# The first stage as one fixed list of named operations, with key reciprocals in PSUM, norms in place and block sums taken from PSUM

## The chip, the cores and the metric

The kernel runs on one core of one Trainium2 chip. The metric is the device time of that core in microseconds; the kernel before has a median of 604.18 us over three runs (603.84 to 605.04 us). A core has five engines with queues of their own: PE (TensorE, matrix products), DVE (VectorE), ACT (ScalarE), POOL (GpSimd) and SP (which here only issues transfers). They share SBUF, the on-chip memory; matrix products are written to PSUM, which has eight banks of 128 x 512 floats. DVE and ACT can read and write PSUM too. Each engine works through its own instructions in program order and waits on semaphores for the others.

## The reference

The input x is 2048 tokens x 512. It is normalised once (xn), and two branches read xn: a linear attention with learned features, and a gated layer.

```python
xn  = (x - mean) / sqrt(var + 1e-5)
q, k, v = xn @ wqkv                        # 32 heads of 16
pq = einsum(q, w_phi); pk = einsum(k, w_phi)     # per head, 16 x 16
phi_q = concat(softmax(pq), softmax(-pq))  # 32 features for each head
phi_k = concat(softmax(pk), softmax(-pk))
kv  = einsum("bhsf,bhsd->bhfd", phi_k, v)  # sums over all tokens
z   = sum over tokens of phi_k
o   = (phi_q @ kv) / (phi_q . z + 1e-6)
s   = o @ wo
gate = xn @ W_gate ; up = xn @ W_up        # 512 x 1376
g   = silu((relu(gate) * up) @ W_down)
out = x + s * g
```

All tokens must have passed through phi_k and v before the first query can be finished, since kv and z are sums over all of them.

## The kernel before, in words

**Arithmetic.** Every fp32 factor of a large product is split into a rounded part (hi, written by ACT as a copy to type fp32r) and a remainder (lo = value - hi, a subtraction on DVE or POOL); three products (lo x hi, hi x lo, hi x hi) replace one. `split` does the two parts and `mm3` the three products. The large products are done as 2 x 2 blocks with seven block products instead of eight: XT, the transposed normalised tokens in SBUF, holds for each block of 128 columns its four blocks A11, A12, A21, A22 and four sums of these, S1 to S4, each as hi and lo.

**Stage 1** (to about 226 us in the profile) works through the 16 token tiles n of 128 tokens. The weights of keys and queries are first multiplied by w_phi (`fold`). Each tile is loaded, normalised, transposed on PE into a bank `pxT`, and split into XT. Its norm is done by `norm_vector` on DVE for tiles 0 to 5; for the others `norm_stats` and `norm_apply` run on ACT and `norm_scale`, three small operations, on POOL. For tiles from 4 on, ACT also copies the transposed tile to SBUF (`full_xt`, tile name `xf`), POOL forms the block sums from two such copies in four operations (`sums_of`, names `sa` and `sb`), ACT rounds them (`sums_hi`) and POOL forms the remainders (`sums_lo`). Keys and values of the first four tiles are plain products (banks `pk`, `pv`). The other twelve tiles go in pairs, the loop `for m in range(2, M)`, e and o being its even and odd tile. One pair is seven block products (to bank `pa`, to the bank `seed` that is kept apart, and to `pd`) and two query products (`query`, bank `pq`), and these steps for each key tile: maximum and minimum of each head (`bounds`, name `mx`), the difference to them for both signs (`shift`, which makes the 128 x 1024 tile `ek`), the exponential on ACT (`expo`), a sum over each group of 16 (`key_total`, name `sm`), the reciprocal of the sums and the scaling of `ek` by it (`key_scale`), the hi and lo parts `phl` (`key_split`; hi on ACT, lo on POOL), an accumulating transfer of `ek` to `zacc`, and eight products with the values (`kv_products`) that accumulate in four banks `pkv` over the whole stage. At the end of the stage `state` gathers these banks, multiplies by a mask (`pkb`, `kvt`) and spreads z (`pz`, `zB`).

**Gate and up.** `gate_up(f)` does one of 11 steps of 128 hidden columns for two blocks of 512 tokens: seven block products again, A11, S2, A12, S3, S1, A22 and, held over to the next step by the list `CARRY`, S4. ACT copies `pa` into `seed`, S2 and then A22 are added to it there, and copies are taken out between them (names `u` and `e`). The hidden values are split into `hh` (hi on ACT, lo on DVE in the first half, on POOL in the second). `down` multiplies them by W_down (bank `py`). The weights of step f are prepared by `f_prep` (ACT, POOL, with the lo parts of f = 0 and 1 on DVE).

**Halves.** Half 0 does steps 0 to 10 for the first 1024 tokens, with queries 0 to 2, the preparation of weights and the products of `down` between; half 1 does the other 1024 tokens with weights fetched back from memory, and queries 3 to 7. The normalised tokens of the second group wait in memory meanwhile (`spill_x`), with `xf` copies of four tiles (`spill_full`).

**What sets the order.** The calls of stage 1 are written out by hand in the order in which each engine gets them. Beside that, a planner (`Clock`, called `pace`) holds generators (weights, queries) and puts their next operation into the program where its own simple count of engine time says that its inputs are there; it is asked after every few products. The preparation of weights for steps 0 and 1 starts at tile 14 (`START = (14, 14)`), and the queries 6 products after step 0 has begun. All instructions are issued by one helper, `InOrder`, so all of them stand at line 51 in the profile, and groups are told apart by the names of their tiles. PSUM is one bank `seed` and a pool `pp` of seven banks that serves all others, four of which `pkv` keeps from the first tile to the end of stage 1. A bank is given to a new tile when the last reader of the old one has finished.

Of the kernel before, what the change touches and what calls it, by code (L numbers as in the profile page):

```python
# [7 lines left out]
F32 = mybir.dt.float32  # L8
# [22 lines left out]
START = (14, 14)  # L31
# [3 lines left out]
A21, A22, A11, A12, S1, S2, S3, S4 = range(8)  # L35

# [111 lines left out]
def layer_kernel(ctx: ExitStack, tc: tile.TileContext, x, wkT, wqT, wv, wo, wf, cst, out):  # L148
# [62 lines left out]
    X = {}  # L211

    def load_x(n):
        b, i = order[n]
        t = b * TPB + i
        X[n] = u2((P, D), "xt")
        nc.sync.dma_start(X[n], x[t * P:(t + 1) * P, :])


    WB, WQ = {}, {}  # L220

    def part(w, name):
        w[name] = u4((P, 2, D), f"{name}h", F32R), u4((P, 2, D), f"{name}l", F32R)
# [8 lines left out]
    def fold(raw, k):  # L232

        p = ps(name="pfold")
        for j in range(KD):
            nc.tensor.matmul(p[:, j * P:(j + 1) * P], raw[k // 2][:, k % 2, j * P:(j + 1) * P], bd_sb[:, j, :],
                             start=True, stop=True)
        return p

    def split_row(w, name, k, src, hi=nc.scalar, lo=nc.vector, turned=True):  # L240

        h, l = (t[:, k, :] for t in w[name])
        if turned:
            h, l, src = by_parity(h), by_parity(l), even_first(src)
        split(h, l, src, lo)


    first = [small(1, name) for name in ("lm", "lv", "lr", "lb")]
    XT = sb.tile([P, 8, 2, 2, BT], F32R, tag="XT", name="XT")
    pace.shared = XT.name  # L250
    XN, XF, SF = {}, {}, {}

    def norm_stats(n):
        xt = X.pop(n)
        xn = u2((P, D), "xn")
        sm, ss, rs, bias = small(1, "lm"), small(1, "lv"), small(1, "lr"), small(1, "lb")
        nc.scalar.activation(xn, xt, AF.Copy, scale=-D ** -1.5, accum_out=sm)
        nc.scalar.activation(xn, xt, AF.Square, bias=sm, scale=D ** -0.5, accum_out=ss)
        XN[n] = xn, xt, bias, rs, sm, ss

    def norm_scale(n):
        xn, xt, bias, rs, sm, ss = XN[n]
        nc.gpsimd.tensor_scalar(rs, ss, 1e-5, None, op0=ALU.add)
        nc.gpsimd.tensor_tensor(rs, rs, mhalf, op=ALU.pow)
        nc.gpsimd.tensor_scalar(bias, sm, rs, D ** 0.5, op0=ALU.mult, op1=ALU.mult)

    def norm_apply(n):
        xn, xt, bias, rs, sm, ss = XN[n]
        nc.scalar.activation(xn, xt, AF.Identity, bias=bias, scale=rs)
        XN[n] = xn  # L270

    def norm_vector(n):

        xt = X.pop(n)
        st, mv, rs = small(6, "bs", 2), small(2, "bm", 2), small(1, "br", 2)
        nc.vector.bn_stats(st, xt)
        nc.vector.bn_aggr(mv, st)
        nc.vector.tensor_scalar(rs, mv[:, 1:2], 1e-5, None, op0=ALU.add)
        nc.gpsimd.tensor_tensor(rs, rs, mhalf, op=ALU.pow)
        XN[n] = u2((P, D), "xn"), xt, mv, rs  # L280

    def norm_vector_apply(n):
        xn, xt, mv, rs = XN[n]
        nc.vector.tensor_scalar(xn, xt, mv[:, 0:1], rs, op0=ALU.subtract, op1=ALU.mult)
        XN[n] = xn
# [4 lines left out]
    def transpose_x(n):  # L290
        p = ps((P, 2, 2, P), name="pxT")
        xn = XN.pop(n)
        for k in range(KD):
            transpose(p[:, k // 2, k % 2, :], xn[:, k * P:(k + 1) * P])
        return p

    def xt_part(n, s):
        a = A21 if n % 2 else A11
        return XT[:, a:a + 2, s, :, cols(n // 2)]

    def hi_xt(n, p):
        nc.scalar.activation(xt_part(n, 0), p, AF.Copy)

    def full_xt(n, p):
        XF[n] = u2((P, 2, 2, P), "xf")
        nc.scalar.activation(XF[n], p, AF.Copy)

    def lo_xt(n, p):
        add(nc.vector, xt_part(n, 1), p, f32(xt_part(n, 0)), ALU.subtract)

    def turn(n, full=True):
        p = transpose_x(n)
        hi_xt(n, p)
        if full:
            full_xt(n, p)
        return n, p

    def sums_of(x0, x1):

        sa, sb_ = u2((P, 2, 2, P), "sa"), u2((P, 2, 2, P), "sb")  # L320
        add(nc.gpsimd, sa[:, 0], x1[:, 0], x1[:, 1])
        add(nc.gpsimd, sb_[:, 0], x0[:, 0], x1[:, 0], ALU.subtract)
        add(nc.gpsimd, sa[:, 1], sa[:, 0], x0[:, 0], ALU.subtract)
        add(nc.gpsimd, sb_[:, 1], x0[:, 1], sa[:, 1], ALU.subtract)
        return sa, sb_

    def sums_x(m):
        SF[m] = sums_of(XF.pop(2 * m), XF.pop(2 * m + 1))

    def sums_hi(m):  # L330
        for s, c in zip(SF[m], (S1, S3)):
            nc.scalar.activation(XT[:, c:c + 2, 0, :, cols(m)], s, AF.Copy)

    def sums_lo(m):
        for s, c in zip(SF.pop(m), (S1, S3)):
            add(nc.gpsimd, XT[:, c:c + 2, 1, :, cols(m)], s, f32(XT[:, c:c + 2, 0, :, cols(m)]), ALU.subtract)
        if m < TPB:
            spill_x(m, 1, 8)

    xt_spill = dram((P, 8, 2, 2, BT), "xts")  # L340
    xf_spill = [dram((P, 2, 2, P), f"xf{n}") for n in range(4)]

    def spill_x(m, a, b):
        nc.sync.dma_start(xt_spill[:, a:b, :, :, cols(m)].rearrange("p c s k t -> p (c s k) t"),
                          f32(XT[:, a:b, :, :, cols(m)].rearrange("p c s k t -> p (c s k) t")))

    def spill_full(n):
        nc.sync.dma_start(xf_spill[n], XF.pop(n))

    def sums_fetch(m):  # L350
        for n in (2 * m, 2 * m + 1):
            XF[n] = u2((P, 2, 2, P), "xf")
            nc.sync.dma_start(XF[n], xf_spill[n])

    def sums_prep(m):
        yield "gpsimd", XF[2 * m + 1]
        sums_x(m)
        for s, c in zip(SF.pop(m), (S1, S3)):
            hi, lo = u2((P, 2, 2, P), "sh", F32R), u2((P, 2, 2, P), "sl", F32R)
            yield "scalar", s  # L360
            nc.scalar.activation(hi, s, AF.Copy)
            yield "gpsimd", hi
            add(nc.gpsimd, lo, s, f32(hi), ALU.subtract)
            for j, t in enumerate((hi, lo)):
                for k in range(2):
                    pace.when(t, lambda c=c, j=j, k=k, t=t: nc.sync.dma_start(
                        xt_spill[:, c:c + 2, j, k, cols(m)], f32(t)[:, :, k]))
        yield None,


    VH, PHI, EK = {}, {}, {}
    PKV, PQ = [], [dram((P, 4, 2, 2 * P), f"pq{h}") for h in range(4)]

    def product(p, a, w, m, first=False):

        c = cols(m)
        hi, lo = WB[w]
        mm3(p, lambda k: (XT[:, a, 0, k, c], XT[:, a, 1, k, c]), lambda k: (hi[:, k, :], lo[:, k, :]), range(2), first)

    def query(h, d, ks=range(KD)):  # L380

        c = slice(h % 2 * 2 * P, (h % 2 + 1) * 2 * P)
        w = slice(d * P, (d + 1) * P)
# [1031 lines left out]
```

## Time and profile before

| | |
|---|---|
| median of three runs | 604.18 us (603.84 to 605.04) |
| the profiled execution, its own time | 607.11 us |
| its span, first to last instruction | 605.3 us |
| mean granted TensorE clock | 0.992 |
| PE busy | 565.1 us (93%) |
| DVE busy | 428.7 us (71%) |
| POOL busy | 407.7 us (67%) |
| ACT busy | 310.1 us (51%) |

Busy times are shares of the span of this one execution; the 1.8 us between its span and its own time lie around the program. A PE record's duration is modelled and overlaps the next record, so the rate of PE is read from the distance of the starts. In the rows of a group, "out<-in" gives the tiles by name, then come partitions x elements, the count, the busy time in us and the mean in ns, and behind the second bar the idle time of that engine just before, with what ended it. In a row of a timeline, the first two numbers are the start and the duration in us.

### The profile page before, as it was taken

To read this page: it belongs to the slowest core of one execution; us is meant where nothing else is said; L and a number is where in the kernel's file an instruction comes from. 1 tells how busy PE (TensorE), PEld (TensorE's weight loads), DVE (VectorE), ACT (ScalarE), POOL (GpSimd) and SP (SyncE) were. 2 spreads that over 40 slices of the span, in tenths; PEclk is the share of its full clock that TensorE was granted. 3 is DMA by queue.
4 is the path that set the end of the run, shared out by engine and by line. 5 is a ranking of instruction groups with operands and counts; after the bars stand their busy time and mean duration, and the time that the engine had idled before them with its cause. 6 is when DMAs were issued, how large, how long until landed. Compare 5 with 4: busy or idle time off the path is not lost. (4 is left out here: it accounts for less than half of the span.)

```text
span 605.3 us, 8090 instructions
## 1 busy us (share of the span) xinstructions
PE 565.1 (93%) x2616; PEld 462.3 (76%) x2616; DVE 428.7 (71%) x536; ACT 310.1 (51%) x557; POOL 407.7 (67%) x339
## 2 busy tenths in 40 slices
PE   7988898889898879999999999999999999999997
PEld 6766676667776758878878878887888878888886
DVE  3996876886999578998898544299899595513322
ACT  2648666767555475754644615143665545542520
POOL 0767777777786449897798913282758869665484
PEclk8999999998999899999999999999999999999999
DMA  8343635522469966788897999999486664558972
GB/s 292 129 156 95 201 90 171 140 70 41 99 179 282 272 226 232 288 297 312 271 354 220 312 303 383 414 383 365 134 268 191 163 220 129 185 192 266 291 240 106
DMA packets 81803, 135.62 MB, mean 224 GB/s; under 512 B 7520, under 2 KB 34528, under 8 KB 80864
## 3 DMA queue, kind: packets, MB, share of 16 engines
q1 hardware_dynamic: 78304, 122.97, 59.3%
q0 software_dynamic: 3312, 12.06, 10.2%
q8 instruction: 21, 0.34, 0.2%
q14 instruction: 22, 0.18, 0.1%
q10 hardware_dynamic: 144, 0.07, 0.0%
HBM read 73.47 MB, written 53.74 MB: 210 GB/s over the span
## 5 line engine op out<-in xcount | busy, mean ns | idle before, releaser
L51 PE MATMUL py<-fd,hh 128*128 128x512 f32 x528 | 130.7, 389 | 0.0
L51 PEld LDWEIGHTS py<-fd,hh 128*128 128x128 f32 x528 | 99.0, 188 | 21.0 <-DVE hh L51 0.4
L51 PE MATMUL seed<-XT,wb 128*128 128x512 f32 x264 | 70.6, 401 | 10.6 <-ACT u L51 6.4
L51 PEld LDWEIGHTS seed<-XT,wb 128*128 128x128 f32 x264 | 48.5, 190 | 26.5 <-ACT u L51 10.7
L51 PE MATMUL pa<-XT,wa 128*128 128x512 f32 x264 | 67.4, 389 | 0.0
L51 PEld LDWEIGHTS pa<-XT,wa 128*128 128x128 f32 x264 | 49.3, 188 | 10.2
L51 POOL TENSOR_TENSOR phl<-ek,phl 128x1024 fp32r<-128x1024 f32 x15 | 35.9, 2392 | 27.5 <-ACT phl L51 27.5
L51 DVE TENSOR_TENSOR y<-py,y 128x512 f32<-128x512 f32 x40 | 27.4, 686 | 24.7 <-PE py L51 24.6
L51 DVE TENSOR_TENSOR e<-pd,e 128x512 f32<-128x512 f32 x22 | 15.0, 684 | 41.6 <-PE pd L51 29.8
L51 DVE TENSOR_TENSOR ek<-ek,sm 128x1024 f32<-128x1024 f32 x15 | 41.7, 2777 | 0.5
L51 POOL TENSOR_TENSOR ez<-eq,zB 128x1024 f32<-128x1024 f32 x16 | 39.4, 2469 | 3.3 <-ACT eq L51 2.5
L51 PE MATMUL pso<-wo,oh 128*128 128x512 f32 (+1 forms) x136 | 39.8, 376 | 0.0
L51 POOL TENSOR_TENSOR y<-y,ys 128x512 f32<-128x512 f32 x24 | 31.1, 1296 | 12.3 <-ACT ys L51 12.3
L51 ACT ACTIVATE seed<-pa 128x512 f32<-128x512 f32 x28 | 16.5, 589 | 40.4 <-PE pa L51 32.5
L51 ACT ACTIVATE hh<-u 128x512 fp32r<-128x512 f32 x22 | 13.9, 632 | 44.7 <-DVE u L51 42.6
L51 POOL TENSOR_TENSOR ol<-of,oh 128x1024 fp32r<-128x1024 f32 x8 | 19.4, 2434 | 24.5 <-ACT oh L51 24.5
L51 PE MATMUL seed<-XT,wc 128*128 128x512 f32 x132 | 33.7, 390 | 0.0
L51 PE MATMUL pd<-XT,wd 128*128 128x512 f32 x132 | 33.7, 389 | 0.0
L51 PE MATMUL pd<-XT,wc 128*128 128x512 f32 x132 | 33.6, 390 | 0.0
L51 DVE TENSOR_TENSOR u<-pd,u 128x512 f32<-128x512 f32 x34 | 23.2, 683 | 13.2 <-PE pd L51 8.4
L51 ACT ACTIVATE phl<-ek 128x1024 fp32r<-128x1024 f32 x15 | 15.9, 1060 | 28.6 <-DVE ek L51 27.6
L51 PEld LDWEIGHTS pso<-wo,oh 128*128 128x128 f32 x136 | 25.0, 188 | 4.8
(224 smaller groups left out, 1484.6 us busy)
## 6 DMA issues: line engine op xcount, KB each, us to landing
zacc<-ek POOLq DMA_DIRECT2D x15, 512.0 KB, 4.5
XT<-xts SPq DMA_DIRECT2D x7, 1024.0 KB, 18.5
rawg<-wf SPq DMA_DIRECT2D x11, 512.0 KB, 3.9
ws<-wa SPq DMA_DIRECT2D x22, 256.0 KB, 3.8
ws<-wb SPq DMA_DIRECT2D x22, 256.0 KB, 5.8
ws<-wc SPq DMA_DIRECT2D x22, 256.0 KB, 5.8
ws<-fd SPq DMA_DIRECT2D x22, 256.0 KB, 3.4
wa<-ws SPq DMA_DIRECT2D x22, 256.0 KB, 4.8
```

Of the source, the lines that this page charges most:

```text
L51: return self.tc.keep_in_program_order(op(*a, **k))
```

## The change

Five things are changed together.

1. **One list.** Stage 1, the gate/up steps f = 0 and 1, the gathering of the state and the preparation of the weights of f = 0, 1 and 2 are now named operations (`op(name, function, tiles)`), and a text `ORDER` lists the names in the order in which they are put into the program. `Plan.run` walks it, asks the planner after each name, and lets a tile go behind the last name that uses it. The planner keeps the rest: queries, which now begin directly behind the list, and the weights from f = 3 on. The key weights are loaded in four pieces. Half 0 starts at f = 2 with the `down` products of f = 0 and 1 waiting.
2. **Key reciprocals in PSUM.** The reciprocal of the sums is written to the first 128 columns of the bank that held the even key (64 for each tile of the pair), and the scaling reads it there. The bank is kept until the odd tile has been scaled.
3. **Norms in place.** The normalised tile overwrites the loaded one. DVE takes the moments of tiles 0 to 3 (before 0 to 5); ACT does the rest; of the small operations only the power stays on POOL, the others move to DVE.
4. **Block sums from PSUM.** DVE forms the four sums from the two transposed banks (one reduction, three additions of 128 x 256). The copies `xf`, the POOL operations `sa` and `sb` and the spills of `xf` are gone; the sums of two blocks are spilled instead. The rounding and the remainder of a block are one operation each of 128 x 1024.
5. **Gate/up step.** `seed` takes S2 alone, DVE adds a copy of A11 to it, a further bank `pc` takes S3 and A22, and DVE adds in place in PSUM. A step has seven DVE operations where it had four, and its copies on ACT fall from three to one (in half 1, for f > 1, two, and one addition on POOL). The order is A11, S2, S3, S1, A22, A12, S4, and nothing is held over. The lo parts of `hh` are all on POOL, as are the lo parts of the weights of f = 0 and 1 and of the differences T2 and T3.

```diff
-START = (14, 14)
+EARLY, BY_VECTOR, IDLE = 3, 4, 8
+ORDER = """
+ld0 bn0 ld1 bn1 lcb lk0 pw0 lk1 ap0 pw1 bi1 T0 ap1 lk2 Fk0 hi0 lo0 T1 kh0 Fk1 hi1 kl0 lo1 kh1 kc0 Fk2 ld3 lk3
...
+class Plan:
+    def run(self, order, after):
+        last = {t: name for name in order for t in self.ops[name][1]}
+        for name in order:
+            fn, tiles = self.ops[name]
+            fn()
+            for t in tiles:
+                if last[t] == name:
+                    self.tiles.pop(t, None)
+            after()
...
-    def key_scale(n):
-        e, pk, sm = EK[n]
-        r = sm if pk is None else pk[:, 0:64]
-        nc.vector.reciprocal(r, sm)
-        nc.vector.tensor_tensor(groups(e), groups(e), r.unsqueeze(2).to_broadcast([P, 64, DH]), op=ALU.mult)
...
+        def r():
+            c = n % 2 * 64
+            return T[bank][:, c:c + 64]
+
+        def total():
+            sm = sb.tile([P, 64], F32, tag="mx", bufs=3, name="sm")
+            nc.vector.tensor_reduce(sm, groups(T[e_]), op=ALU.add, axis=AX.X)
+            nc.vector.reciprocal(r(), sm)
...
+        op(f"sc{n}", lambda: nc.vector.tensor_tensor(groups(T[e_]), groups(T[e_]), r().unsqueeze(2).to_broadcast([P, 64, DH]),
+                                                     op=ALU.mult), e_, bank)
...
-    def sums_of(x0, x1):
-        sa, sb_ = u2((P, 2, 2, P), "sa"), u2((P, 2, 2, P), "sb")
-        add(nc.gpsimd, sa[:, 0], x1[:, 0], x1[:, 1])
-        add(nc.gpsimd, sb_[:, 0], x0[:, 0], x1[:, 0], ALU.subtract)
-        add(nc.gpsimd, sa[:, 1], sa[:, 0], x0[:, 0], ALU.subtract)
-        add(nc.gpsimd, sb_[:, 1], x0[:, 1], sa[:, 1], ALU.subtract)
-        return sa, sb_
...
+        def sums():
+            x0, x1, s = T[e], T[o], u4((P, 4, 2, P), "sums")
+            T[s_] = s
+            nc.vector.tensor_reduce(s[:, 0], x1.rearrange("p h k t -> p k t h"), op=ALU.add, axis=AX.X)
+            add(nc.vector, s[:, 1], s[:, 0], x0[:, 0], ALU.subtract)
+            add(nc.vector, s[:, 2], x1[:, 1], s[:, 1], ALU.subtract)
+            add(nc.vector, s[:, 3], x0[:, 1], s[:, 1], ALU.subtract)
...
+            op(f"hS{m}", lambda: nc.scalar.activation(part(0), T[s_], AF.Copy), s_)
+            op(f"slo{m}", lambda: add(nc.gpsimd, part(1), T[s_], f32(part(0)), ALU.subtract), s_)
...
     def gate_up(f, ...):
         pa = ps(name="pa")
         mm3(pa, w_of(f, 0, 0), a_of(A11), range(2))
-        pb = seed
-        nc.scalar.activation(pb, pa, AF.Copy)
-        mm3(pb, w_of(f, 1, 0), a_of(S2), range(2), first=False)
-        nc.scalar.activation(m, pb, AF.Copy)
+        nc.scalar.activation(t1, pa, AF.Copy)
+        mm3(pb, w_of(f, 1, 0), a_of(S2), range(2))
+        add(nc.vector, m, pb, t1)
+        pc = ps(name="pc")
+        mm3(pc, w_of(f, 1, 1), a_of(S3), range(2))
...
+            add(nc.vector, e7, pc, m)
...
+        add(nc.vector, pc, pc, m)
...
-            queries = pace.add(all_queries(0), 6)
+            queries = pace.add(all_queries(0), 0, 1.5)
-        for f in range(NF):
+        for f in range(0 if half else 2, NF):
-            run(gate_up(f, nc.gpsimd if half else nc.vector, used, rest))
+            run(gate_up(f, half and f > 1, used, lambda: again and f_reload(f + 1, 1)))
```

The number of matrix products hardly changes (2,566 instructions before, 2,567 after); what moves is what stands between them. Three places show it.

First DVE in the middle of the pair loop. Before, the row in which the even tile of a pair is summed and scaled stands among the splits of XT, and the scale reads `sm` in SBUF:

```order
L51 TENSOR_REDUCE sm<-ek 128x64
L51 TENSOR_TENSOR XT<-pxT,XT 128x2x2x128
L51 RECIPROCAL sm<-sm 128x64
L51 TENSOR_TENSOR ek<-ek,sm 128x1024
L51 TENSOR_REDUCE mx<-pa 128x32 x2
L51 TENSOR_TENSOR ek<-pa,mx 128x1024
```

After, the reciprocal goes to the bank `pa`, the scale reads that bank, and the block sums of the next pair (from `pxT`) have joined the row:

```order
L103 TENSOR_REDUCE sm<-ek 128x64
L103 RECIPROCAL pa<-sm 128x64
L103 TENSOR_TENSOR ek<-ek,pa 128x1024
L103 TENSOR_TENSOR u<-pd,u 128x512
L103 TENSOR_REDUCE sums<-pxT 128x256
L103 TENSOR_TENSOR sums<-sums,pxT 128x256
L103 TENSOR_TENSOR sums<-pxT,sums 128x256 x2
L103 TENSOR_TENSOR XT<-pxT,XT 128x2x2x128 x2
```

What moved: the reciprocal follows its sum at once, one operand of the scale has changed its memory, and four operations of 128 x 256 are new here.

Second POOL in one pair. Before, the four sums of a block and the three small operations of one norm (`lr` and `lb`):

```order
L51 TENSOR_TENSOR sa<-xf 128x256
L51 TENSOR_TENSOR sb<-xf 128x256
L51 TENSOR_TENSOR sa<-sa,xf 128x256
L51 TENSOR_TENSOR sb<-xf,sa 128x256
L51 TENSOR_SCALAR lr<-lv 128x1
L51 TENSOR_TENSOR lr<-lr,mhalf 128x1
L51 TENSOR_SCALAR lb<-lm,lr 128x1
```

After, from the one small operation that a norm still has on POOL to the remainder of the block sums:

```order
L103 TENSOR_TENSOR lr<-lr,mhalf 128x1
L103 TENSOR_TENSOR phl<-ek,phl 128x8x128
L103 DMA zacc<-ek 128x1024
L103 TENSOR_TENSOR vhl<-u,vhl 128x8x64
L103 TENSOR_TENSOR XT<-sums,XT 128x4x2x128
```

What moved: the four sums and two of the three small operations of a norm are gone from POOL, and the remainder of the block sums is one row instead of two.

Third PE where gate/up step 0 runs. Before, behind the last query product (`pq`), S2 (`seed`, from `wb`), A12 (`pa`) and S3 (`seed` again) follow each other, and products of the last keys (`pkv`) come in the middle of S3:

```order
L51 MATMUL pq<-XT,1h 128x512 x2
L51 MATMUL seed<-XT,wb 128x512 x6
L51 MATMUL pa<-XT,wa 128x512 x6
L51 MATMUL seed<-XT,wb 128x512 x3
L51 MATMUL pkv<-phl,vhl 128x256 x8
```

After (the banks of the step are named `ga`, `gc`, `gd` here), products of the last keys and a query product of 12 stand around S2, and S3 goes to `gc` only behind that query:

```order
L103 MATMUL ga<-XT,wa 128x512 x6
L103 MATMUL pkv<-phl,vhl 128x256 x8
L103 MATMUL seed<-XT,wb 128x512 x6
L103 MATMUL pq<-XT,WQ0l 128x512
L103 MATMUL pq<-XT,WQ0h 128x512 x2
```

What moved: S3 goes to a bank of its own and `seed` is not used twice in the row, and query products of the last pairs have moved into the gate step.

1023 lines of the change are left out of this document (500 added, 523 removed).

## The prediction

> **What bounds the kernel now.** I read the shares of the engines first, then the slices of the span, then the span by stages.
>
> ```profile
> PE 565.1 (93%) x2616; PEld 462.3 (76%) x2616; DVE 428.7 (71%) x536; ACT 310.1 (51%) x557; POOL 407.7 (67%) x339
> PE   7988898889898879999999999999999999999997
> ```
>
> PE is the busiest engine, but its slices hold 7 and 8 in the first fifteen and 9 afterwards. Each slice is 15.1 us, so the weak part ends at about 226 us. The view by stages (start and end, length, then busy time of PE, weight loads, DVE, ACT and POOL, and the granted clock) gives it its size:
>
> ```profile
> 0.00:8.20 8.20, 4.40 (x16) 3.17 (x16) 2.10 (x10) 1.28 (x1) 0.75 (x5) 1.00 0.69 225
> 8.20:61.10 52.90, 46.74 (x244) 38.35 (x245) 42.58 (x59) 34.31 (x66) 33.25 (x29) 0.97 0.48 161
> 61.10:187.70 126.60, 110.76 (x526) 89.61 (x526) 102.17 (x99) 80.07 (x149) 95.33 (x97) 0.99 0.49 128
> 187.70:226.30 38.60, 31.22 (x139) 24.50 (x137) 27.11 (x43) 21.50 (x49) 18.90 (x18) 0.96 0.85 261
> 226.30:400.00 173.70, 172.35 (x773) 141.26 (x774) 127.29 (x164) 84.47 (x147) 124.00 (x106) 1.00 0.90 312
> 400.00:605.30 205.30, 199.62 (x923) 165.44 (x921) 127.42 (x164) 88.42 (x147) 135.47 (x87) 1.00 0.68 218
> ```
>
> The rows are the opening (two), the six pairs, the first gate steps with the state, and the two halves. PE idles 3.8 + 6.2 + 15.8 + 7.4 = 33.2 us before 226.3 us, and 1.4 + 5.7 = 7.1 us after it. So the change can win only ahead of 226 us; behind it, it can only lose.
>
> Busy time hides part of a stall, since the last record in front of a wait runs out alone. A count against the steady distance of the starts is better. The chain of waits, where PE is the limit, shows it: six products of 512 columns take 1.36 us (0.227 each), eight of 256 take 0.97 us (0.121 each).
>
> ```profile
> 514.89 1.36 PE pa L51 x6
> 527.16 0.97 PE pnum L51 x8
> 105.38:127.65 22.27, 18.69 (x91) 14.98 (x91) 16.87 (x17) 15.02 (x30) 16.44 (x19) 1.00 0.38 95
> 122.44 0.60 PE L51 MATMUL pxT<-ident,xn 128*128 128x128 f32 x4
> ```
>
> The third row is one pair of the loop: 66 products of 512 columns, 16 of 256 and 8 transposes (0.60 us for four, less the overlapping end, about 0.11 each) are 15.0 + 1.9 + 0.9 = 17.8 us of work in 22.27 us. The two last pairs have no transposes, 16.9 us each. Six pairs are 4 x 17.8 + 2 x 16.9 = 105.0 us of work in 126.6 us: 21.6 us of stall. DVE and POOL are busy 16.9 and 16.4 us in a pair, less than PE's work: neither is full, so it is the order of dependencies that costs. The waits in stage 1 name it (engine, what waits, on whom, us in total, times, longest):
>
> ```profile
> PE pkv L51 <- POOL phl L51: 8.8, 5, 2.0
> PE seed L51 <- ACT u L51: 6.2, 5, 2.2
> PE pa L51 <- DVE XT L51: 3.7, 4, 1.5
> PE pxT L51 <- DVE xn L51: 3.3, 4, 1.0
> PE pfold L51 <- DMA wkT<-wkT: 2.4, 1, 2.4
> PE seed L51 <- ACT seed L51: 2.0, 1, 2.0
> ACT phl L51 <- DVE ek L51: 27.6, 14, 3.1
> POOL phl L51 <- ACT phl L51: 27.5, 14, 2.3
> ```
>
> PE waits for `phl` on POOL, that one for ACT, that one for the scaling of `ek` on DVE. One such chain in the timeline of a pair:
>
> ```profile
> 106.86 1.58 POOL L51 TENSOR_TENSOR XT<-sa,XT 128x512 fp32r<-128x512 f32 x1
> 106.94 3.84 DVE L51 TENSOR_TENSOR ek<-ek,sm 128x1024 f32<-128x1024 f32 x1
> 108.13 1.56 POOL L51 TENSOR_TENSOR XT<-sb,XT 128x512 fp32r<-128x512 f32 x1
> 110.88 1.06 ACT L51 ACTIVATE phl<-ek 128x1024 fp32r<-128x1024 f32 x1 [1.74 <-DVE ek L51]
> 112.01 2.35 POOL L51 TENSOR_TENSOR phl<-ek,phl 128x1024 fp32r<-128x1024 f32 x1 [2.33 <-ACT phl L51]
> 114.42 1.22 PE L51 MATMUL pkv<-phl,vhl 128*128 128x256 f32 x8 [1.95 <-POOL phl L51]
> ```
>
> The scale ends 1.09 us after POOL's `XT<-sb` does (110.78 against 109.69), as if it began its work only then.
>
> **The change, part by part.** The reciprocal in PSUM first. The scale before, and the only scale of the same shape whose second operand lies in PSUM, in the queries:
>
> ```profile
> L51 DVE TENSOR_TENSOR ek<-ek,sm x15: 1225/2446/3879, 43.2 to 194.0; 128x1024 f32<-128x1024 f32 x15
> L51 DVE TENSOR_TENSOR eq<-eq,qr x16: 1206/1214/1224, 245.5 to 517.6; 128x1024 f32<-128x1024 f32 x16
> L51 DVE TENSOR_TENSOR ek<-ek,sm 128x1024 f32<-128x1024 f32 x15 | 41.7, 2777 | 0.5
> ```
>
> The query's never exceeds 1.22 us although POOL is 71% busy around it (124.0 of 173.7), the key's reaches its 1.23 us only at best and is 2.78 us in the mean. Sixteen at 2.78 - 1.21 = 1.57 us are 25 us of DVE, 3.1 us in each pair. Bounds: nothing, if it stays at 2.78, and this whole; I take the whole, since shape and operands are those of the queries.
>
> The other edits by rows of their shapes:
>
> ```profile
> L51 DVE TENSOR_REDUCE mx<-pa 128x32 f32<-128x512 f32 x12 | 7.7, 676 | 0.0
> 212.84 0.42 DVE L51 TENSOR_TENSOR kvt<-pkb,pm 128x256 f32<-128x256 f32 x1
> L51 ACT ACTIVATE xf<-pxT 128x512 f32<-128x512 f32 x16 | 9.5, 595 | 0.0
> L51 POOL TENSOR_TENSOR XT<-sa,XT 128x512 fp32r<-128x512 f32 x6 | 9.2, 1538 | 0.1
> L51 POOL TENSOR_TENSOR sa<-xf 128x256 f32<-128x256 f32 x8 | 5.9, 740 | 0.4
> L51 DVE TENSOR_TENSOR T2l<-wvr,T2h 128x512 fp32r<-128x512 f32 x2 | 3.5, 1786 | 0.0
> L51 POOL TENSOR_TENSOR hh<-e,hh 128x512 fp32r<-128x512 f32 x11 | 14.6, 1325 | 11.1 <-DMA wb<-ws 7.0 <-ACT hh L51 3.3 <-DMA od<-eq 0.8
> L51 DVE TENSOR_TENSOR u<-pd,u 128x512 f32<-128x512 f32 x34 | 23.2, 683 | 13.2 <-PE pd L51 8.4 <-ACT xn L51 2.1 <-ACT u L51 1.8
> L51 POOL TENSOR_TENSOR phl<-ek,phl 128x1024 fp32r<-128x1024 f32 x15 | 35.9, 2392 | 27.5 <-ACT phl L51 27.5
> ```
>
> Block sums: DVE gets 8 x (0.68 + 3 x 0.42) = 15.5 us; ACT loses 16 copies (9.5 us); POOL loses the eight sets of four operations (about 24 us for all) and, in six blocks, two remainders of 1.54 us for one of about 2.4 us (the row of `phl`), 6 x 0.7 = 4 us. For POOL that is 28 us less in stage 1. It takes over the lo parts of T2 and T3 (4 x 1.3 = 5.3 us), of four splits of `hh` (5.3 us) and of the weights of f = 0 and 1 (for each, four of 128 x 512 at 1.3 and one of 128 x 256 at 0.74, 12.1 us for both), and all POOL work on the weights of f = 2 (those five and four sums of 0.74, 9.0 us): 32 us, most of it late in the stage, so about 4 more in all. DVE sheds 4 x 1.79 = 7 us for T2 and T3, and 6 us or more for the weights. The norms in place and the moved small operations change a pair by under 1 us on each engine, and one idle product and three more issues on SP lie in the opening, ahead of the first weights and under the loads. In a pair DVE so goes from 16.9 to 16.9 - 3.1 + 1.9 + 0.4 = 16.1 us (0.4 for small operations of the norms), POOL from 16.4 by -3.0 (sums) -0.7 -0.5 to 12.2 us, against 17.8 us of PE.
>
> Now what this is worth on the path, stage by stage.
>
> - Pairs: 21.6 us of stall. The chain to `phl` gets 1.6 us shorter for each of two keys, and the row also parts the products from what they wait for: in the list, the sum, the scale, `phl` and the `pkv` products of a key stand many products apart. If all waits vanished it would be -21.6; if only the scale shrank, the 8.8 us of `pkv` waits go and -8.8 is left. I take -16: nearer to the full gain, as no engine but PE has more than 16.1 us of work in a pair; 5.6 us stay, for handovers of banks (below).
> - Opening: 10.0 us idle in two rows, of which the loads before 8.2 us keep at least 3. POOL, DVE and ACT are not full (42.6 us of 52.9 for DVE), but the new order gives ACT the norms of tiles 1 to 5, and its share rises. I take -4, between 0 and -7.
> - Steps 0 and 1, state: 7.4 us idle and a clock of 0.96 in 38.6 us (1.5 us). The two waits on ACT for `seed` (6.2 and 2.0 us) come mostly from here and lose their reason, since S2 starts a fresh group and S3 has a bank of its own; queries stand between. I take -6, between -2 and -9.
> - Behind: both halves have more small work. Half 0: POOL gets 18 lo parts of 1.3 us (23.6 us) and loses the weights of f = 2 (9 us): 124.0 to about 139 of 173.7 us. DVE swaps those 18 lo parts for 27 additions of 0.68 us, about even. Half 1: DVE gets at most 33 of 0.68 us, 22 us, to 150 of 205.3. PE covers both. PE there waits on ACT before `seed`:
>
> ```profile
> PE seed L51 <- ACT u L51: 2.3, 5, 0.9
> PE seed L51 <- ACT seed L51: 2.1, 3, 1.4
> ```
>
> These 4.4 us go, but the start of S2 in the next step now needs DVE's addition from `seed`, and a third bank is held through a step. I take +1, between -4 and +8 (22 steps by one wait of about 0.4 us, near the mean of the first row).
>
> Sum: -16 - 4 - 6 + 1 = -25 us on a span of 605.3, so about 580 us of span. The profiled execution took 607.11 us, 1.8 more than its span, and lies 2.9 us above the median of 604.18 us; taken from the median, -25 gives 579 us (0.958 of before).
>
> **Banks.** Four of the seven pooled banks are kept for `pkv`, so three serve `pa`, `pd`, `pxT` and `pq`. Before, `pa` is let go when the even key has been shifted, after the products A11, a query, S2 and A12 (30 x 0.227 = 6.8 us and a shift). After, it is held until the scale of the odd key, about a pair's work, some 22 us. So two banks are left for 6 `pd`, 12 `pq` and 8 `pxT`; with 6 `pa` these are 32 handovers, each of which can stall PE until ACT or DVE has emptied the bank. My sum has 5.6 us for them. The Trainium skill, Perfetto Trace Analysis, section Optimization Strategy, says that gaps which repeat on the engine that should be saturated can mean that SBUF or PSUM does not suffice for the next tile. By that page the gaps of the pairs would stay with this change, and the sum would be -25 + 16 = -9 us, or grow. The trace of before does not bear it out there: the repeating gap, 1.95 us in front of `pkv`, ends with POOL's `phl` and not with a bank.
>
> **Rivals.**
>
> 1. Banks run short (same or slower). Nearest rows for one handover are PE's waits on ACT for `seed`, 1.2 us in the mean and 2.2 at most. The gain is used up at 25 / 32 = 0.8 us each; at 1.2 us the time is 579 + 38 = 617 us. For it: two banks for 26 tiles. Against it: queries and transposes are emptied by operations of 0.6 us while 6 to 12 other products run (1.4 to 2.7 us).
> 2. Only the scale helps (smaller gain). The list trades one wait for another, ACT in the opening, DVE's row in the pairs: -8.8 in pairs, -2 for steps 0 and 1, nothing else, 604.2 - 10.8 = 593 us. For it: DVE still has 16.1 us in a pair of 17.8.
> 3. The halves give it back. POOL at 139 of about 170 us and a bank less: +0.5 us in 22 steps, 11 us, 590 us.
> 4. The scale stays at 2.8 us, as something other than the memory of `sm` slows it (the row of 106.94 speaks against): DVE in a pair then has 19.2 us, above PE's 17.8, and six pairs take at least 6 x 19.2 = 115.2 us; with the forecast's 105 + 5.6 us for the pairs, 579 + 4.6 = 584 us or more.
>
> **How the numbers follow.** Forecast 0.66, its own range 569 to 587 (by terms -21, -6, -8, 0 and -12, -2, -4, +1 from the median). Banks 0.10 (two thirds of it slower), only the scale 0.13, the halves 0.08, scale unchanged 0.03. The time of the likeliest is 579. The range 562 to 598 takes in the second, third and fourth with their ends, the lowest sum (-21.6 -7 -9 -4 = -42, 562) and the milder cases of banks, and leaves out the rest of those and the slow end of the halves. The runs of before lie within 0.2%, which is about what can be told from no change. Slower: banks at over 0.8 us, 0.07, and the third far beyond its price, 0.03, together 0.10; same 0.02; faster 0.88.
>
> **What the next profile would show.** `ek<-ek,pa` with a mean near 1.21 us; the first `py` product at about 200 us instead of 226; no wait of PE on `phl` above 1 us; a pair in 18 to 19 us; slices of 9 from the third on. Wrong if PE waits in front of `pxT`, `pq` or `pd` on the readers of the old bank (rival 1), if POOL is above 90% in half 0 or PE waits on DVE in front of `seed` (rival 3), or if the first stage ends later than 215 us.

## The result, and the profile after

The changed kernel takes 579.33 us in the median (578.32 to 582.18, four runs) against 604.36 us for the kernel before: a ratio of 0.959, 95% interval 0.956 to 0.963. The forecast was 579 us. The profiled execution took 582.18 us, its span is 580.4 us; it lies 2.9 us above its median, as that of before did, so the spans of 605.3 and 580.4 us can be compared.

The engine shares and PE's slices:

```profile
PE 564.5 (97%) x2618; PEld 464.5 (80%) x2618; DVE 423.1 (73%) x601; ACT 290.8 (50%) x511; POOL 429.2 (74%) x325
PE   8999999979999999999998999999999999999997
```

The view by stages, cut where the pairs begin (50.88 us; 61.1 before), at the first product of the gate steps (160.5 us; 187.7 before) and at the first `py` product (197.9 us; 227.80 before), columns as in the prediction:

```profile
0.00:8.20 8.20, 6.23 (x25) 4.99 (x26) 3.27 (x11) 2.35 (x3) 1.56 (x6) 1.00 0.69 209
8.20:50.88 42.68, 42.68 (x232) 36.36 (x232) 38.30 (x71) 38.10 (x79) 33.15 (x25) 1.00 0.62 213
50.88:160.50 109.62, 105.12 (x504) 86.82 (x503) 86.51 (x126) 75.00 (x130) 82.13 (x63) 0.97 0.58 147
160.50:197.90 37.40, 36.74 (x179) 30.16 (x178) 19.84 (x33) 17.67 (x42) 30.77 (x28) 1.00 0.86 273
197.90:400.00 202.10, 197.12 (x866) 159.80 (x865) 153.76 (x203) 80.38 (x136) 146.07 (x118) 0.99 0.89 309
400.00:580.40 180.40, 176.58 (x819) 146.39 (x817) 121.38 (x160) 77.28 (x125) 135.53 (x88) 1.00 0.66 202
```

From 8.2 us to the first pair PE is busy throughout, and the weak part of the slices is gone but for one 7 (the ninth, 116 to 131 us). Counting the starts of PE's products against the steady distance (226.7 ns for 512 columns, 119.5 for 256, 111 for 128) splits each stage into work, distances that are too long by less than 25 ns, and stalls (anything longer, except some products at half the rate, 2 to 4 us in all). The rows also leave out 1.5 us ahead of the first product and 4 us behind the start of the last:

| us | length before / after | work | long distances | stalls |
|---|---|---|---|---|
| to the first pair | 61.1 / 50.9 | 44.5 / 44.8 | 0 / 0.1 | 12.6 / 2.9 |
| to the first `py` | 166.7 / 147.1 | 134.1 / 135.3 | 0.2 / 1.7 | 31.5 / 9.9 |
| to the end | 377.5 / 382.5 | 366.0 / 364.6 | 0.8 / 5.3 | 6.4 / 8.0 |

Ahead of the first `py` 29.9 us are won, behind it 5.0 us are given back. Of what is given back, 4.5 us are a slower steady rate, which the prediction did not have at all. PE's waits that are left (engine, what waits, on whom, us, times, longest):

```profile
PE pd L103 <- DVE XT L103: 3.5, 1, 3.5
PE pc L103 <- DVE e L103: 2.4, 3, 1.9
PE pnum L103 <- DVE pTl L103: 2.2, 2, 1.8
PE seed L103 <- DVE idle L103: 1.5, 1, 1.5
PE seed L103 <- ACT seed L103: 1.0, 1, 1.0
```

No wait on `phl` is among them, and the scale has its forecast price (first its group, then the one wait of the pairs that is left, in the timeline):

```profile
L103 DVE TENSOR_TENSOR ek<-ek,pa x12: 1210/1220/1221, 67.1 to 163.6; 128x1024 f32<-128x1024 f32 x12
```

```profile
119.69 0.88 POOL L103 DMA_DIRECT2D zacc<-ek  x1 [3.21 <-DVE ek L103]
...
128.20 0.69 DVE L103 TENSOR_REDUCE sums<-pxT 128x256 f32<-128x512 f32 x1 [4.87 <-DMA zacc<-ek]
...
130.95 0.77 PE L103 MATMUL pd<-T1h,XT 128*128 128x512 f32 x1 [3.49 <-DVE XT L103]
```

The block sums are to go into a buffer that held an `ek`, which the accumulating transfer issued at 119.69 still reads; DVE stands for 4.9 us, the bank of the transposed tile is not emptied, and PE waits 3.5 us for that bank. PE waits for the reader of the old bank, as in rival 1, once; but what made that reader late is a buffer in SBUF and not a shortage of banks.

The wait costs more than its 3.5 us. From 131.0 to 135.6 us the granted clock is 0.50, and behind the wait eleven distances of starts in a row are 0.43 us, where 0.227 is the steady one, 2.2 us more in all:

```profile
134.08 0.63 PE L103 MATMUL seed<-T4l,XT 128*128 128x512 f32 x1
134.50 1.05 PE L103 MATMUL seed<-T4h,XT 128*128 128x512 f32 x2
135.36 0.63 PE L103 MATMUL seed<-T4l,XT 128*128 128x512 f32 x1
```

In the table these 2.2 us are among the 9.9 us of stalls.

### The profile page after: what moved, and what is told of

It reads as the page before. It is cut to its first block, busy times and chain, and to the rows that moved or that the text cites. A ratio compares the mean times of both kernels' runs of the same rounds, so it can differ in the third digit from the quotient of the medians.

```text
span 580.4 us, 8064 instructions
## 1 busy us (share of the span) xinstructions
PE 564.5 (97%) x2618; PEld 464.5 (80%) x2618; DVE 423.1 (73%) x601; ACT 290.8 (50%) x511; POOL 429.2 (74%) x325
## 4 chain that ended last, share of the span: by engine, by line
PE 46%; DVE 3%; POOL 3%; issue 1%; DMA 1%; SPq 0%; ACT 0%; DVEq 0%; POOLq 0%
PE py L103 14%; PE pso L103 8%; PE pc L103 7%; PE pa L103 6%; PE pd L103 6%; PE seed L103 3%; PE pnum L103 2%; DMA od<-eq 1%; DVE y L103 1%; DVE qd L103 1%; POOL hh L103 0%; POOL fd L103 0%; POOL sl L103 0%; POOL ez L103 0%; DVE eq L103 0%
## 5 line engine op out<-in xcount | busy, mean ns | idle before, releaser
L103 PEld LDWEIGHTS py<-fd,hh 128*128 128x128 f32 x528 | 99.1, 188 | 21.8
L103 PE MATMUL pa<-XT,wa 128*128 128x512 f32 x240 | 62.7, 395 | 0.0
L103 POOL TENSOR_TENSOR hh<-e,hh 128x512 fp32r<-128x512 f32 x20 | 26.0, 1299 | 41.4 <-ACT hh L103 41.4
L103 ACT ACTIVATE hh<-e 128x512 fp32r<-128x512 f32 x20 | 12.6, 632 | 51.9 <-DVE e L103 42.7
L103 POOL TENSOR_TENSOR ol<-of,oh 128x1024 fp32r<-128x1024 f32 x8 | 19.2, 2402 | 21.8 <-ACT oh L103 17.2
L103 PE MATMUL pc<-XT,wc 128*128 128x512 f32 x120 | 32.7, 399 | 2.4 <-DVE e L103 2.4
L103 PE MATMUL seed<-XT,wb 128*128 128x512 f32 x132 | 34.3, 395 | 0.0
L103 POOL TENSOR_TENSOR hh<-u,hh 128x512 fp32r<-128x512 f32 x20 | 25.9, 1295 | 8.4 <-ACT hh L103 8.3
L103 PE MATMUL pc<-XT,wb 128*128 128x512 f32 x120 | 31.9, 400 | 0.0
L103 DVE TENSOR_TENSOR y<-pso,y 128x512 f32<-128x512 f32 (+1 forms) x15 | 9.8, 656 | 27.6 <-PE pso L103 27.6
L103 ACT ACTIVATE eq<-pnum 128x512 f32<-128x512 f32 x32 | 17.4, 593 | 24.3 <-PE pnum L103 24.3
L103 PEld LDWEIGHTS seed<-XT,wb 128*128 128x128 f32 x132 | 24.7, 188 | 5.9
```

The source lines that it names most:

```text
L103: return self.tc.keep_in_program_order(op(*a, **k))
```

## The experiments

Ratios are to the kernel before in the same session, with 95% intervals.

### Reciprocals alone: out of the new kernel, into the old one

In the changed kernel, reciprocals in SBUF:

```diff
         def r():
-            c = n % 2 * 64
-            return T[bank][:, c:c + 64]
+            c = n % 4 * 64
+            return zraw[:, c:c + 64]
...
```

`zraw` is the buffer `zB` in SBUF, which is unused until the end of the stage. The bank of the even key is held as long as before.

> The changed kernel with the key reciprocals written to SBUF (room that is unused until the end of the stage) and read there by the scale; list, norms, sums and gate steps as changed. Theory (the scale's operand in PSUM is needed for the gain): the scale returns to about 2.5 us or more, DVE gets some 20 us back, about 3 us for each pair, more than PE's slack: 584 to 591 us. Rival (the list alone carries the gain, the reciprocal is hidden): 578 to 581 us. If the scale stays at 1.2 us, its price was never the operand but what ran beside it.

Measured: 580.70 us, 0.962 (0.957 to 0.967), 1.4 us above the change, with intervals that overlap. Its scale:

```profile
L103 DVE TENSOR_TENSOR ek<-ek,zB 128x1024 f32<-128x1024 f32 x16 | 31.0, 1949 | 0.3
```

Sixteen times 0.73 us more of DVE than in the change (1949 against 1217 to 1220 ns), 12 us, are all but hidden. The rival holds.

In the kernel before, reciprocals in PSUM:

```diff
-    key_shift(0, pk)
+    key_shift(0, pk, r=pk)
...
-        key_shift(e, pa)
+        key_shift(e, pa, r=pa)
...
-        key_shift(o, seed, mx)
+        key_shift(o, seed, mx, pa[:, 64:128])
```

> The kernel before with the key reciprocals in PSUM (in the bank of the even key, held until the odd key's scale), everything else as before. Theory (by the prediction's price for the scale alone): the scale takes 1.21 us, PE's waits on phl, 8.8 us, mostly go: 593 to 597 us. Rival a (the waits only change their name, since the order is the cause): 602 to 605 us. Rival b (the reciprocal is nearly the whole change): 580 to 585 us. Rival c (held banks stall PE): over 606 us.

Measured: 606.51 us, 1.004 (1.002 to 1.007): slower by 0.4%, just inside rival c, held banks. The scale takes 1.22 us there, and no wait on `phl` is among the largest, but others have come:

```profile
PE pq L51 <- DVE XT L51: 6.4, 4, 1.6
PE pk L51 <- DVE XT L51: 4.9, 1, 4.9
...
PE pa L51 <- ACT pqs L51: 2.6, 4, 0.7
```

A query product reads blocks of XT that were split long before. What it waits for is the bank of `pxT`, whose last reader is that split, and `pa` waits for the bank of `pq`: with `pa` held there is no bank to spare in the old order.

The stages say where the loss lies. The first pair begins at 67.96 us (61.14 before), for the edit also holds the banks `pk` of the plain keys in the opening, and the 4.9 us stand there:

```profile
55.81 0.80 PE L51 MATMUL pk<-B11h,XT 128*128 128x512 f32 x1 [4.91 <-DVE XT L51]
```

From the first pair to the first `py` this run takes 162.1 us where the kernel before takes 166.7, with the same work. So in these two executions the shorter scale is worth 4.6 us to the old pairs, about half of the 8.8 us of waits on `phl`, and the opening loses 6.8.

### The distance between a key and its products

Only the list is changed: each `kv` of tiles 4 to 15 moves to directly behind `pl` (or `vl`) of its tile, as here for tile 11.

```diff
-P5.5 z11 ex10 aw5 pq5.1 ph11 P1.6 pl11 kv8 cS6
+P5.5 z11 ex10 aw5 pq5.1 ph11 P1.6 pl11 cS6
...
-T15 z10 hi14 sums7 P3.6 vl11 P7.6 lo14 P5.6 pl10 sq4.0 hi15 cW6 lo15 P4.6 kv11
+T15 z10 hi14 sums7 P3.6 vl11 kv11 P7.6 lo14 P5.6 pl10 sq4.0 hi15 cW6 lo15 P4.6
...
```

> The changed kernel with one thing moved in the list: the products of keys and values of tiles 4 to 15 stand directly behind the remainder phl of the same tile (or behind the value's, where that comes later), instead of 0 to 12 us of products further on. Nothing else differs. Theory (the gain comes from the distance between a key's scale and its products): PE waits for phl again, 2 us or more at each of eight to twelve tiles, 595 to 610 us. Rival (PE had no need of the distance, the gain lies in the other engines' orders): 579 to 583 us.

Measured: 581.99 us, 0.961 (0.958 to 0.965). PE waits for `phl` again, but only twice:

```profile
PE pkv L102 <- POOL phl L102: 3.3, 2, 2.0
```

The theory falls: the distance to the products is by itself worth about 3 us (the intervals of this run and of the change overlap), not 16 or more.

### The order of the pairs

The pairs 3 to 7 of the list in the sequence of the kernel before, with the operations as changed:

```diff
-P1.3 sq2.1 z3 lpm st13 au2 ap8 kv2 ex4 st10 sh5 bi11 sm4 q3.0 cS3 ex5 ep10 P6.3 pl3 vh5 P3.3 ...
+P1.3 cS3 ph4 pl4 z4 q3.1 pq3.1 sq3.1 P6.3 cU3 ph5 pl5 st10 ep10 pw10 bi10 P3.3 kv4 mx6 sh6 ...
```

> The changed kernel with the pairs m = 3 to 7 of the list put back into the sequence that the kernel before has written out by hand (one pair ends before the next begins, each query where it stood, weights of f = 0 to 2 from the last pair on); the opening, the gate steps and all operations themselves as changed. Theory (the list's order of the pairs carries their gain; the parts alone gained nothing in the old order): the stall of these pairs returns, 12 us or more, 591 to 600 us. Rival (the parts carry it: reciprocals and block sums in PSUM shorten what a pair waits for, whatever the order): 579 to 584 us.

Measured: 632.45 us, 1.045 (1.041 to 1.049), 53 us above the change and 27 above the kernel before; the first `py` comes at 244.89 us. The waits:

```profile
PE pa L102 <- DVE XT L102: 14.3, 4, 3.7
PE pd L102 <- DVE w L102: 7.0, 3, 2.9
...
PE ga L102 <- POOL wa L102: 4.7, 1, 4.7
PE gd L102 <- POOL wc L102: 4.1, 1, 4.1
PE seed L102 <- POOL wb L102: 3.1, 1, 3.1
PE pxT L102 <- ACT pqs L102: 2.7, 4, 0.7
```

The first row is the handover of a bank again (`pa` takes the one of `pxT`, which DVE empties after the block sums), 3.6 us in each of four pairs; the second is S4 waiting until DVE has taken S1 out of `pd`. Behind each of the four waits for `pa`, nine to twelve products follow at about 0.43 us (granted clock 0.54 from 73.7 to 80 us), another 8.8 us in all. Some 12 us (`ga`, `gd`, `seed`) come from where I put the weights of the gate steps, not from the pairs. Without them, by subtraction, some 40 us remain. So with the new operations this order is far worse than the old kernel, and rival 1 describes the larger part of it that has a name: 17.0 us of handovers (`pa`, `pxT`) with those 8.8 us, beside 7.0 us for `pd`.

### Block sums as before, in the new list

```diff
-            nc.vector.tensor_reduce(s[:, 0], x1.rearrange("p h k t -> p k t h"), op=ALU.add, axis=AX.X)
-            add(nc.vector, s[:, 1], s[:, 0], x0[:, 0], ALU.subtract)
...
+            nc.scalar.activation(x0, T[e], AF.Copy)
+            nc.scalar.activation(x1, T[o], AF.Copy)
+            add(nc.gpsimd, s[:, 0], x1[:, 0], x1[:, 1])
+            add(nc.gpsimd, s[:, 1], s[:, 0], x0[:, 0], ALU.subtract)
...
```

> The changed kernel with the block sums made as before (each transposed tile copied to SBUF by ACT, four operations on POOL), everything else as changed, the list too. Theory (the list was made for room that the sums in PSUM opened; the kernel with three parts undone stalled as much in stage 1 as the kernel before, and the reciprocals alone cost it 1.4 us): 12 us or more in stage 1, 591 us or more. Rival (each part alone is hidden by the list, only both together were too much): 580 to 585 us.

Measured: 606.77 us, 1.002 (1.000 to 1.004): the whole gain is gone. The first `py` comes at 223.41 us. In the first 51 us of this kernel the waits that head the list and answer to the edit are:

```profile
DVE XT L103 <- ACT xf L103: 7.3, 2, 4.8
...
PE pv L103 <- POOL B12l L103: 5.0, 2, 3.7
...
POOL sums L103 <- ACT xf L103: 3.7, 2, 2.7
```

DVE waits for ACT's copies, POOL's row waits too, and PE waits for a weight behind POOL's sums. Stalls ahead of the first `py` rise from 12.8 to 38.7 us by the count of starts. In one point this is not the kernel before: there POOL forms the sums of the first two blocks only in half 0 (its last `sa` starts at 332.9 us), here within the opening. The first pair begins at 60.38 us, 9.5 us later than in the change; the other 16 us by which the first `py` is late lie in the pairs and the first gate steps.

Three parts undone together (reciprocals in SBUF with the bank freed early, block sums on POOL, the old gate step), list kept:

> The changed kernel with three parts undone at once: reciprocals in SBUF with the bank of the even key free after its shift, block sums from ACT copies on POOL, and the old gate/up step from f = 2 on and in half 1. The list stays, with the norms in place and its own two gate steps. Theory after the first runs (the distances in the list carry the gain, the rest is hidden): 578 to 585 us. Rival (the parts each open room that the list needs, since DVE and POOL are near their limit in the pairs): 590 us or more.

Measured: 632.55 us, 1.045 (1.040 to 1.051). This kernel, and the next one, fetch the block S4 back one step early at the end of half 0, so that one product reads the wrong tokens and waits 8 to 9 us for the transfer; their times are too long by that. Ahead of it they can be read: the first `py` comes at 230.73 us, later than in the kernel before. This list, with the three old operations in it and the first two blocks' sums on POOL in the opening (first pair at 61.7 us), gains nothing.

### The gate/up step

```diff
-            run(gate_up(f, half and f > 1, used, lambda: again and f_reload(f + 1, 1)))
+            run(gate_up(f, nc.gpsimd if half else nc.vector, used, lambda: again and f_reload(f + 1, 1)))
```

(with the old `gate_up`, `finish_f` and `CARRY` in place of the new).

> The changed kernel with the old gate/up step (copies through seed, S4 held over, lo parts of half 0 on DVE) from f = 2 on and in half 1; list, reciprocals, sums as changed. Theory (the new step neither gains nor loses in the halves): 577 to 581 us. Rival by the prediction's third rival (the new step's extra work on POOL and DVE costs in the halves): 574 us or less. Other rival (the new step saves the 4.4 us of waits for seed): 583 us or more.

Measured: 601.78 us, 0.993 (0.990 to 0.996), burdened as said. With the block fetched back at its time:

> As the run with the old gate/up step from f = 2 on, but with the block S4 of XT fetched back at the end of half 0 behind its last use, where that run fetched it back one step early, so that PE waited 8.2 us for the transfer there. Theory (the new step is worth something in the halves, since in the old one ACT's copies to seed are late again, 8.6 us in seven waits in that run): 587 to 594 us. Rival (nearly all of that run's loss was the early transfer): 578 to 583 us.

Measured: 590.29 us, 0.975 (0.969 to 0.982), 11 us above the change (10 by the ratios). The first `py` comes only 2.0 us later (199.95), and the waits for the copies are back:

```profile
PE seed L103 <- ACT seed L103: 8.4, 7, 2.6
```

The two profiled executions differ by 7.3 us (span 587.7). Of these, 2.0 lie ahead of the first `py` and 3.5 are stalls behind it; what makes the medians differ by 11 is not settled.

The new step alone, in the kernel before:

> The kernel before with the new gate/up step in all steps of both halves (S2 alone in seed, a bank pc, additions on DVE, nothing held over, lo parts of half 0 on POOL); stage 1 as before. Theory: the waits of steps 0 and 1 on ACT for seed (about 5 us) go, and nothing else: 597 to 602 us. Rival (the new step needs the list around it): 604 us or more.

Measured: 609.25 us, 1.006 (1.003 to 1.009). The rival holds: its first `py` is 1.1 us earlier (226.69), and stalls behind it grow from 6.4 to 11.2 us. Among its waits is the new bank's:

```profile
PE pc L51 <- DVE e L51: 5.3, 3, 3.4
```

### The slower rate: where the tiles lie

Three groups of products in half 1, first of the kernel before, then of the change. Six products take from one start to the next 1.36 us there, 1.40 here:

```profile
454.25 1.52 PE L51 MATMUL pa<-XT,wa 128*128 128x512 f32 x6
455.61 1.52 PE L51 MATMUL seed<-XT,wb 128*128 128x512 f32 x6
456.97 1.52 PE L51 MATMUL py<-fd,hh 128*128 128x512 f32 x6
```

```profile
473.89 1.56 PE L103 MATMUL seed<-XT,wb 128*128 128x512 f32 x6
475.29 1.56 PE L103 MATMUL pc<-XT,wb 128*128 128x512 f32 x6
476.69 0.63 PE L103 MATMUL py<-fd,hh 128*128 128x512 f32 x2
```

The kernel before had four small tiles (`first`, 384 bytes) ahead of XT; the change removes them. So XT and the ring of 2 KB tiles now begin 128 bytes past a multiple of 512, while the 4 and 8 KB tiles begin at one. In the kernel before all began at one.

Put back in the changed kernel, with other small tiles ahead of XT:

```diff
+    spare = [sb.tile([P, 64], F32, tag="mx", bufs=3, name="sm"), small(2, "bm")]
+    mhalf = sb.tile([P, 8], F32, name="mhalf")[:, 0:1]
     XT = sb.tile([P, 8, 2, 2, BT], F32R, tag="XT", name="XT")
...
+    zB = small(256, "zB", 1).rearrange("p (d x) -> p d x", d=4)
+    spare += [u8((P, KD, D), "spare"), u4((P, 2, D), "spare")]
+    spare.clear()
```

> The changed kernel with XT and the 2 KB buffers moved so that all large tiles begin at a multiple of 512 bytes, as before the change (in the changed kernel XT and the 2 KB ring begin 128 bytes past one, the larger tiles at one). No instruction is added or taken away. In its profile the starts of 512-column products that read XT lie 230 to 233 ns apart, in the profile before 227; summed over the program that is 7.1 us. Theory (place in memory): the distance returns to 227 ns and the time falls by 6 to 8 us, to about 572 us. Rival (denser work, or more PSUM traffic, slows each product): distance and time stay, 579 us within 1.5.

Measured: 576.42 us, 0.954 (0.951 to 0.958), 2.9 us below the change, with intervals that overlap at their ends. The distance is back:

```profile
468.96 1.52 PE L103 MATMUL seed<-XT,wb 128*128 128x512 f32 x6
470.32 1.52 PE L103 MATMUL pc<-XT,wb 128*128 128x512 f32 x6
471.68 1.52 PE L103 MATMUL py<-fd,hh 128*128 128x512 f32 x6
```

And the other way round, XT alone shifted in the kernel before:

```diff
-    first = [small(1, name) for name in ("lm", "lv", "lr", "lb")]
     XT = sb.tile([P, 8, 2, 2, BT], F32R, tag="XT", name="XT")
+    first = [small(1, name) for name in ("lm", "lv", "lr", "lb")]
```

> The kernel before with XT alone moved from a multiple of 512 bytes to 128 bytes past one (four small tiles stand behind XT instead of ahead of it). Nothing else differs. Theory (place in memory): the distance of products that read XT rises from 227 to about 232 ns and the time by 5 to 9 us, to 609 to 613 us. Rival (denser work): 604 us, distance 227.

Measured: 607.95 us, 1.005 (1.002 to 1.008).

```profile
448.19 1.55 PE L51 MATMUL pa<-XT,wa 128*128 128x512 f32 x6
449.58 1.56 PE L51 MATMUL pd<-XT,wd 128*128 128x512 f32 x6
450.98 1.56 PE L51 MATMUL seed<-XT,wb 128*128 128x512 f32 x6
```

The place in memory is the cause of the slower rate, shown in both directions. The sum of the long distances is about 7 us each time, the time moves by about 3 us: less than the 6 to 8 and 5 to 9 us expected. In this run the stalls are 5 us fewer than before, so that a slower PE seems to wait less elsewhere.

### A version that beats both

The aligned kernel, with the one wait of the pairs moved away by one name of the list:

```diff
-P5.5 z11 ex10 aw5 pq5.1 ph11 P1.6 pl11 kv8 cS6 ap14 P2.5 spill3 P6.6 sm10 sc10 T14 rw1 ap15 ph10 cU6 au5 vh11
-T15 z10 hi14 sums7 P3.6
+P5.5 z11 ex10 aw5 pq5.1 ph11 P1.6 pl11 kv8 cS6 ap14 P2.5 spill3 P6.6 sm10 sc10 T14 ap15 ph10 cU6 au5 vh11
+T15 z10 hi14 sums7 rw1 P3.6
...
```

> The changed kernel with all large tiles at a multiple of 512 bytes (as in the run with them aligned) and one name of the list moved: rw1, the load of the raw weights of f = 1, behind sums7 instead of ahead of it. With that the tile of the block sums takes a buffer whose last reader is PE, where it took one that an accumulating transfer still read (the profile after shows DVE idle for 4.9 us there, and PE 3.5 us). Theory: 2 to 4 us below the aligned kernel, 572.5 to 574.5 us. Rival (the transfer is then waited for elsewhere): 576 us.

Measured: 573.78 us, 0.948 (0.945 to 0.951), clear of the change's interval. It touches that of the aligned kernel (0.951 to 0.958), so that the 2.6 us of the moved name alone are likely and not shown. In its profile the wait has all but gone, and with it the half rate behind it (granted clock 1.00 from the first pair to the first `py`, 0.98 in the change):

```profile
PE pd L103 <- DVE XT L103: 0.2, 1, 0.2
```

## Why the prediction was right, and where it was not

The time was right (579.33 for 579) and the stages came out as forecast in sign. The reason given first did not hold, and that the middle of the forecast was met is luck: the errors of four terms cancel.

- **Where the loss lay.** Right: 29.9 us were won ahead of the first `py` and 5.0 lost behind it.
- **The scale.** Its duration was right (1.22 for 1.21 us). Its value was not. The step that failed is "the chain to `phl` gets 1.6 us shorter for each of two keys", which I had carry part of the 16 us of the pairs, with 8.8 as the worth of the scale alone in rival 2. Undone in the new kernel it costs 1.4 us. Alone in the old one it wins 4.6 us in the pairs and loses 6.8 in the opening, as the waits on `phl` turn into waits for banks.
- **The distance in the list.** I had `phl` and the `pkv` products "many products apart" as the second half of that step. Moved next to each other, `phl` and its products cost about 3 us. The slow scale and the short distance were not put into one kernel; that each makes up for the lack of the other is not ruled out.
- **What stands in their place.** Block sums undone take the whole gain away, and the order of the pairs undone takes about 40 us, with banks as the largest named part. I had priced the block sums at nothing on the path, as 15.5 us of DVE against 28 of POOL. The 28 were misread as well: two of the eight sets lie in half 0, so stage 1 sheds six sets, about 18 us, and the 4 us of remainders, 22. The parts do not add up (27 and 40 us, with 11 for the gate step, against a gain of 25): each is measured in a list that was made for all of them. That this list needs the new sums and the new operations need an order other than that of the old pairs is shown; whether another list could carry the old sums, and what the new sums are worth in the old kernel, is not. The norms in place were not undone.
- **Terms.** Counted by the starts, the pairs lose 21.8 - 9.6 = 12.2 us of what is not work (forecast 16) and the first gate steps, up to the first `py`, 11.0 - 2.4 = 8.6 (forecast 6). The opening was mis-sized: -4 forecast, 10.2 us earlier measured, outside its bounds of 0 and -7, which kept at least 3 us for the loads where 2.0 us stay idle in the first row. Behind: +1 forecast, +5.0 measured, of which 4.5 by the count are the rate that comes with XT's place (the whole time moves by 2.9 us when it is put back). By length, 6.2 us more from the opening covered 2.4 us less from the next two stages (22 forecast, 19.6 measured, as 1.2 us of work moved into them) and 4.0 us more lost behind. Of the opening's edits only the block sums were undone apart: 9.5 of the 10.2 us go with them, though POOL then has two blocks more there than in the kernel before.
- **Rivals.** The banks came true in the old order, not in the list: one handover of 3.5 us is left, with 2.2 us of half rate behind it. The rule of the Trainium skill (Perfetto Trace Analysis, section Optimization Strategy) that repeating gaps can mean too little SBUF or PSUM, which I weighed against the change, fits the reciprocals alone in the kernel before (four waits of `pq`, 6.4 us) and the old order of pairs (four of `pa`, 14.3 us), and not the change itself, where the gap comes once. That only the scale helps is wrong: in the new kernel it is worth 1.4 us. The halves: POOL is busy 146.1 of 202.1 us from the first `py` to 400 us, far from the 90% that was to speak for that rival, and the new step, in the new kernel, saves time (about 11 us) where I had it cost 1.
- **The chance.** One result cannot say whether "faster" at 0.88 was right. Two of the parts alone, the reciprocals and the gate step, are slower than before, and so are the new operations with the order of the old pairs: the gain hung on parts that I had not priced as hanging together.

## What to carry to other kernels

A stall that a profile names (here PE on `phl`, 8.8 us) is the last of several that lie close behind each other; before it is priced as a gain, ask which wait ends second, and count the banks that the remedy holds. Undo parts within the new kernel as well as adding them to the old one: both tests of the reciprocals were needed to see that they carry little in the new order, and in the old one win in the pairs what they lose in the opening. Price a wait of PE together with the slow products behind it (3.5 and 2.2 us here). And compare the steady distance of PE's products between two kernels, not only their waits: a changed distance shows a cost that no list of waits has.

## What the runs showed of the hardware that I had not expected

Products whose operands include XT follow each other at 226.7 ns when all large tiles begin at a multiple of 512 bytes. When XT begins 128 bytes past one and the weights at one, they follow at 231.4 to 233.6 ns in the mean (`wa`, `wb` and `wc`, change, 400 to 500 us); with `wb` it is 233.3, alternating near 229 and 237.5. In the change the product of S4, whose weights `wd` lie 128 bytes past too, has 228.2 ns there; with XT alone shifted it has 233.3. That suggests that the places of the two operands against each other count and not either by itself, but its neighbours in the row differ as well, and it was not tried apart. Neighbours do count: `py`, both of whose operands begin at a multiple, takes 231.1 ns for the first product of a group and 226.9 for the fifth in the change, 227.1 and 226.8 in the aligned kernel.
